# Refill loads of twice the size for experts two to seven of a soft MoE, with joined tiles

## The chip, the cores and the metric

The kernel runs on one core of a Trainium2 chip. The metric is the device time of one execution in microseconds (us). A core has five engines with one instruction queue each: TensorE (PE in the profile), VectorE (DVE), ScalarE (ACT), GpSimd (POOL) and SyncE (SP). SyncE computes nothing here: it issues every transfer of the kernel, in program order. The transfers themselves are carried by the core's 16 DMA engines.

## The reference

An attention with a sigmoid in place of the softmax feeds a soft mixture of experts. All data are float32.

```python
scores = q @ k.T / sqrt(64) - log(448)          # 8 batches, 12 heads, 448 tokens, 64 wide
x = (sigmoid(scores) @ v)                       # -> 3584 tokens x 768
logits = x @ phi                                # 768 -> 32 slots (8 experts x 4)
slot_input = softmax over tokens(logits).T @ x  # 32 x 768
for e in range(8):
    h = relu(slot_input[e] @ w1[e])             # 4 x 768 @ 768 x 1024
    slot_out[e] = h @ w2[e]                     # 4 x 1024 @ 1024 x 768
out = softmax over slots(logits) @ slot_out     # 3584 x 768
```

## The kernel before, in words

**Two parts.** For about 280 us TensorE computes the attention, batch after batch, and folds each finished batch of x into the slot inputs. Weights of the experts are loaded meanwhile, one or two units at a time. Then the experts run (`w1_part`, line 616; `w2_step`, line 730), and the output rows are made and stored (`out_half`, `out_rows`, `out_rows2`, lines 694 to 712).

**Units.** The weights come in 128 units of 128 partitions by 768 floats (3,072 bytes a partition): 64 of w1, eight per expert, and 64 of w2, two per call of `w2_step`. `units` (line 91) is the order in which they are loaded. The first 70 units, which hold all of w1 and six units of w2, are loaded during the attention. The other 58, all of w2, find no free room until w1 has been used: they are the refills, and they overwrite places that w1 (and the turned x, below) held.

**Places.** `slots` (line 98) lists the places in the order in which units take them, and later, in the same list, the order in which the output tiles take them. Before the change, a place `wa0` to `wa12` has four units. Besides there are `wpe` (four), `wpx` (two), `wpy` (four) and the tiles `wc` (two each).

**Refills.** `w1_part(e)` multiplies expert e by the two halves of its w1 (four units each). After each half it calls `load(4)` on the place that the half has just freed. The first refill goes into `wa0` in three pieces (lines 131 and 132), then come twelve loads of four units into `wa1` to `wa12`, one into `wpe`, all from the input `wq`, and one of two units into `wpx` from `wz`. A partition's line in `wq` is 12,288 bytes long. SyncE issues these loads, then the 23 stores of the output in program order.

**Who reads what.** Number the 32 calls of `w2_step` 0 to 31: 0 to 15 make the left half of the output's columns (pass 0), 16 to 31 the right half (pass 1). Step n reads two units. Steps 0 to 2 read the `wc` tiles. `wa0` holds the units of steps 3 and 4, `wa1` those of 5 and 6, and so on: `waN` those of 2N+3 and 2N+4, up to `wa12` with 27 and 28. `wpe` holds 29 and 30, `wpx` 31. Steps 20 to 27 are each followed by one `out_half` of the left half, which can run since `spread_sum` (line 721) has made pass 0's result ready after step 19. After step 31 the chain of line 718, `spread_sum` again, and the products of line 691 makes the other stores: two `out_rows`, five `out_rows2`, eight `out_half` of the right half.

**Turned x.** During the attention, the last 16 units' worth of the `wa` places hold not weights but the 32 by 32 transposed x (`yy`, line 165), and some columns for the slot softmax (`t1e`). Weights are loaded into them when the slot products (line 391) and line 418 have read them. `wpe` holds x and turned x of some batches (`xe`, `y0`, `y1`, line 171).

**Transfers in order.** A transfer waits at SyncE until its place is free. Each transfer raises one of eight semaphores in turn, so that the ninth transfer waits until the first has landed. This wait stands in the trace as SyncE at line 134 waiting for a DMA.

Of the kernel before, what the change touches and what calls it, by code (L numbers as in the profile page):

```python
# [9 lines left out]
F32 = mybir.dt.float32  # L10
# [7 lines left out]
DM, NSLOT, E, SPE, F = 768, 32, 8, 4, 1024  # L18
P = 128
# [10 lines left out]
UNIT = 768  # L30
N_A = 52
N_X = 16
N_1 = N_A - N_X + 2
N_C = 4
N_F = 70
# [22 lines left out]


@with_exitstack  # L60
def soft_moe_attention(ctx: ExitStack, tc: tile.TileContext, qk, v, vl, phi, w, wq, wz, cst, out):
    nc = tc.nc
    ctx.enter_context(tc.manual_schedule(engines=MANUAL))

# [2 lines left out]
    wpa = ctx.enter_context(tc.tile_pool(name="wpa", bufs=1))  # L67
# [23 lines left out]
    units = [(u1, u2)[m][n] for m, a, b in ORDER for n in range(a, b)]  # L91
    state = {"next": 0, "ring": 0, "used": 0, "room": 0, "wpb": None}
    utile, quads = {}, {}
    wpe, wpx, wpy = (wpa.tile([P, n * UNIT], F32, name=name) for name, n in (("wpe", 4), ("wpx", 2), ("wpy", 4)))

    wa_slots = [("wa", n, 0, 4) for n in range(N_A // 4)]
    n1 = (N_A - N_X) // 4
    slots = wa_slots[:n1] + [(wpy, 0, 0, 2)] + wa_slots[n1:] + [(wpe, 0, 0, 4), ("wc", 0, 0, 2), (wpx, 0, 0, 2)]
    slots += [("wc", n, 0, 2) for n in range(1, N_C)] + [(wpy, 0, 2, 4)]
    slots += wa_slots + [(wpe, 0, 0, 4), (wpx, 0, 0, 2), (wpy, 0, 0, 4)] + wa_slots  # L100

    def ring_tile(size=1):
        while state["used"] + size > state["room"]:
            pool, n, used, room = slots[state["ring"]]
            state.update(ring=state["ring"] + 1, used=used, room=room)
            if pool == "wa":
                pool = wpa.tile([P, 4 * UNIT], F32, name=f"wa{n}")
            elif pool == "wc":
                pool = state["wpb"].tile([P, 2 * UNIT], F32, name=f"wc{n}")
            state["tile"] = pool  # L110
        t = state["tile"][:, state["used"] * UNIT:(state["used"] + size) * UNIT]
        state["used"] += size
        return t

    def load(size):
        n = state["next"]
        if n >= len(units):
            return
        state["next"] = n + size
        if n < N_F:  # L120
            src, m = w[n // 2], n % 2 * UNIT
        elif n < len(units) - 2:
            src, m = wq[(n - N_F) // 4], 0
        else:
            src, m = wz[0], 0
        t = quads[(0, 0)] if n == N_F else ring_tile(size)
        if n < N_F and units[n][0] == "w1" and units[n][2] == 0 and units[n][1] < E - 1:
            quads[units[n][1:4:2]] = state["tile"]
        if n == N_F:
            state["ring"] += 1  # L130
            for a in range(0, 4 * UNIT, 4 * 256):
                nc.sync.dma_start(t[:, a:a + 4 * 256], src[:, a:a + 4 * 256])
        else:
            nc.sync.dma_start(t, src[:, m:m + size * UNIT])
        for k in range(size):
            utile[units[n + k]] = t[:, k * UNIT:(k + 1) * UNIT]
# [6 lines left out]
    def w1_mm(ph, e, kcs):  # L143
        for kc in kcs:
            for j in range(4):
                if e < E - 1:
                    wt = quads[(e, kc // TR)][:, (kc % TR * 4 + j) * 256:(kc % TR * 4 + j + 1) * 256]
                else:
                    wt = utile[("w1", e, j, kc // TR)][:, kc % TR * 256:(kc % TR + 1) * 256]
                nc.tensor.matmul(  # L150
                    ph[32 * j:32 * j + 32, 0:256], phi_sb[:, kc, :], wt,
                    start=(kc == 0), stop=(kc == NKC - 1))

    with ExitStack() as actx:
# [5 lines left out]
        def hold(kind, n=""):  # L160
            return ap.tile(kinds[kind], F32, name=f"{kind}{n}")

        wx = [wpa.tile([P, 4 * UNIT], F32, name=f"wa{(N_A - N_X) // 4 + n}") for n in range(N_X // 4)]
        ny = TR * NB2 * P
        yy = [w4[:, 0:ny].rearrange("p (k c f) -> p k c f", k=TR, c=NB2) for w4 in wx]
        t1e = [w4[:, ny:ny + NB2 * NSLOT + 1] for w4 in wx]
# [1 line left out]
        held = {k: hold(*k) for k in (("qk", 0), ("qk", 1), ("v", 0))}  # L168
        vlt = ap.tile([P, P], F32, name="vl")[:]
        held.update({k: hold(*k) for k in (("qk", 2), ("att", 0), ("att", 1), ("att", 2), ("v", 1))})  # L170
        yf = [wpe[:, 0:2 * UNIT], wpe[:, 2 * UNIT:4 * UNIT], wpy[:, 2 * UNIT:4 * UNIT]]
        xe = [y[:, 0:TR * S].rearrange("p (k s) -> p k s", k=TR) for y in yf]
        y0, y1, yn = (y.rearrange("p (k c f) -> p k c f", k=TR, c=NBK) for y in yf)
        xy = ap.tile([P, TR * NBK * P], F32, name="xy")
# [378 lines left out]
        for i in range(len(seq) + LAG):  # L553
            for f in early.get(i, ()):
                f()
            if i < len(seq):
                u = seq[i]
                score(u)
                if u[1] == NFK:
                    load_qk(u[0] + 3)  # L560
                elif u[0] % 2 == 1 and u[1] == NFK - 1:
                    load_qk(u[0] + 3)
                while state["next"] < min(N_1, (i + 1) * N_1 // W_STEPS):
                    load(1)
                if state["next"] < N_1 + N_X and (i > NX0 and i % 2 == 1 and state["next"] < N_1 + N_X // 2 or i > NX1):
                    load(1)
                if i == (B - 1) * per_b + LAG + LAST_S:
                    load(2)
                    load(2)
# [39 lines left out]
    def av_tile(name):  # L609
        turn[name] += 1  # L610
        return ps_av.tile([P, 512], F32, name=f"{name}{turn[name] % 2}")

    for _ in range(N_C + 2):
        load(2)

    def w1_part(e, ph=None):
        if ph is None:
            ph = av_tile("av0")
            w1_mm(ph, e, range(TR))
        if e < E - 1:  # L620
            load(4)
        if e == 0:
            finish(ps_t)
        w1_mm(ph, e, range(TR, NKC))
        load(min(4, len(units) - state["next"]))
        return ph

    def h_part(e, ph):
# [65 lines left out]
    def out_half(m, hf):  # L694
        ov = ring_tile().rearrange("p (j c) -> p j c", j=2)
        for j in range(2):
            out_tile(ov[:, j, :], m + j, hf, j)
        nc.sync.dma_start(
            out[m * ROWS:(m + 2) * ROWS, hf * HALF:(hf + 1) * HALF].rearrange("(j p) c -> p j c", p=P), ov)

    def out_rows(m):
        ov = ring_tile().rearrange("p (j c) -> p j c", j=2)
        for hf in range(2):
            out_tile(ov[:, hf, :], m, hf, hf)
        nc.sync.dma_start(out[m * ROWS:(m + 1) * ROWS, :].rearrange("p (j c) -> p j c", j=2), ov)
# [39 lines left out]
    for e in range(E):  # L745
        ph = w1_part(e, ph0 if e == 0 else None)
        if prev is not None:
            h_part(*prev)
        prev = (e, ph)
        combine_softmax(e)  # L750
# [67 lines left out]
```

## Time and profile before

| what | value |
|---|---|
| median of 3 runs | 370.95 us (370.52 to 371.78) |
| the profiled execution | 371.16 us |
| its span, first to last instruction | 369.4 us |
| TensorE busy in the span | 346.2 us (94%) |
| mean granted TensorE clock | 0.981 |
| HBM read, written | 83.59 MB, 11.01 MB |

The span is what the hardware profiler saw from the first to the last instruction of one execution. The profiled execution is 1.76 us longer than its span, and 0.21 us longer than the median. In the rows below, a time is counted from the start of the span. A line that begins with a start time is a merged piece of a timeline: start, duration, what it is, how many instructions, and in brackets what the engine was idle for just before. PE counts two records for one float32 matmul: one `w2_step` of four matmuls is `x8`.

### The profile page before, as it was taken

To read this page: it belongs to the slowest core of one execution; us is meant where nothing else is said; L and a number is where in the kernel's file an instruction comes from. 1 tells how busy PE (TensorE), PEld (TensorE's weight loads), DVE (VectorE), ACT (ScalarE), POOL (GpSimd) and SP (SyncE) were. 2 spreads that over 40 slices of the span, in tenths; PEclk is the share of its full clock that TensorE was granted. 3 is DMA by queue.
4 is the path that set the end of the run, shared out by engine and by line. 5 is a ranking of instruction groups with operands and counts; after the bars stand their busy time and mean duration, and the time that the engine had idled before them with its cause. 6 is when DMAs were issued, how large, how long until landed. Compare 5 with 4: busy or idle time off the path is not lost.

```text
span 369.4 us, 10332 instructions
## 1 busy us (share of the span) xinstructions
PE 346.2 (94%) x4315; PEld 172.0 (47%) x4315; DVE 241.2 (65%) x614; ACT 222.0 (60%) x305; POOL 8.2 (2%) x36
## 2 busy tenths in 40 slices
PE   9999999999999999999999999999999988996840
PEld 5566655644444355444444644464557643422520
DVE  0158829796894986769859695989746782141650
ACT  5777777577777765777777387747672114421540
POOL 1000000000000000000000000000102000100000
PEclk9999999999999999999999999999999999999895
DMA  7666566465677663766566388739689999999997
GB/s 230 222 217 209 182 221 217 141 216 172 211 227 219 201 199 98 227 212 197 190 215 230 92 293 262 238 110 373 231 285 369 428 421 422 424 422 405 395 409 282
DMA packets 34494, 95.27 MB, mean 258 GB/s; under 512 B 3600, under 2 KB 17296, under 8 KB 32784
## 3 DMA queue, kind: packets, MB, share of 16 engines
q1 hardware_dynamic: 34448, 94.62, 73.1%
q8 instruction: 34, 0.56, 0.6%
q14 instruction: 12, 0.10, 0.1%
HBM read 83.59 MB, written 11.01 MB: 256 GB/s over the span
## 4 chain that ended last, share of the span: by engine, by line
PE 78%; DMA 14%; DVE 3%; ACT 0%; issue 0%; DVEq 0%; ACTq 0%; SPq 0%
PE sc L234 34%; PE av L275 33%; DMA wpx<-in_wz_dram 8%; DMA wa<-in_wq_dram 6%; PE av L150 3%; PE sc L391 2%; PE sc L337 2%; DVE wa L692 2%; DMA qk<-in_qk_dram 1%; PE sc L319 1%; PE av L250 1%; PE pt L691 1%; PE av L391 0%; PE av L691 0%; PE av L723 0%
## 5 line engine op out<-in xcount | busy, mean ns | idle before, releaser
L242 ACT ACTIVATE att<-sc,sm 128x896 f32<-128x896 f32 x167 | 167.8, 1007 | 80.6 <-PE sc L234 77.3
L234 PE MATMUL sc<-qk 64*64 64x448 f32 x1336 | 180.0, 538 | 0.1
L275 PE MATMUL av<-att,v 64*64 64x448 f32 x1128 | 152.7, 537 | 0.0
L234 PEld LDWEIGHTS sc<-qk 64*64 64x64 f32 x1336 | 61.2, 133 | 71.0 <-issue 58.1
L275 PEld LDWEIGHTS av<-att,v 64*64 64x64 f32 x1128 | 54.5, 133 | 54.3 <-issue 52.6
L300 DVE STREAM_TRANSPOSE wa<-wpe 32x384 f32<-32x384 f32 (+5 forms) x144 | 58.0, 403 | 2.2
L300 DVE STREAM_TRANSPOSE wa<-xy 32x192 f32<-32x192 f32 (+3 forms) x96 | 33.1, 345 | 1.6
L282 DVE TENSOR_TENSOR wpe<-wpe,av 128x448 f32<-128x448 f32 x18 | 11.2, 621 | 31.3 <-PE av L275 20.1
L275 PE MATMUL av<-att,vl 64*64 64x448 f32 x188 | 26.4, 537 | 0.0
L300 DVE STREAM_TRANSPOSE wa<-wpx 32x288 f32<-32x288 f32 (+1 forms) x48 | 25.0, 520 | 0.8
L282 DVE TENSOR_TENSOR wpx<-wpx,av 128x448 f32<-128x448 f32 x15 | 9.3, 621 | 19.7 <-PE av L275 17.5
L150 PE MATMUL av<-wa,jt 128*32 128x256 f32 x312 | 17.2, 380 | 0.2
L692 ACT COPY wa<-av 128x384 f32<-128x384 f32 x24 | 10.9, 479 | 9.1 <-PE av L691 8.6
L692 DVE COPY wa<-pt 128x384 f32<-128x384 f32 x24 | 12.6, 555 | 5.5 <-PE pt L691 5.2
L282 DVE TENSOR_TENSOR xy<-xy,av 128x448 f32<-128x448 f32 x14 | 8.7, 622 | 8.2 <-ACT xy L278 4.1
L275 PEld LDWEIGHTS av<-att,vl 64*64 64x64 f32 x188 | 9.2, 133 | 9.2 <-issue 9.0
L150 PEld LDWEIGHTS av<-wa,jt 128*32 128x32 f32 x312 | 10.1, 110 | 6.7 <-issue 0.3
L691 PE MATMUL av<-lt,wc 128*128 128x384 f32 x28 | 12.5, 447 | 0.5 <-DVE lt L726 0.5
L691 PE MATMUL pt<-lt,wc 128*128 128x384 f32 x28 | 10.5, 377 | 1.1 <-DVE lt L726 1.1
L300 DVE STREAM_TRANSPOSE wpe<-xy 32x256 f32<-32x256 f32 (+3 forms) x32 | 11.0, 345 | 0.5
L633 ACT COPY t<-tmp 128x32 f32<-128x32 f32 x8 | 1.7, 217 | 15.7 <-DVE tmp L631 15.7
L740 PE MATMUL av<-wa,jt 128*32 128x384 f32 x104 | 10.2, 493 | 1.0 <-DMA wa<-in_wq_dram 1.0
(171 smaller groups left out, 262.8 us busy)
## 6 DMA issues: line engine op xcount, KB each, us to landing
qk<-in_qk_dram SPq DMA_DIRECT2D x47, 448.0 KB, 3.7
wa<-in_w_dram SPq DMA_DIRECT2D x52, 384.0 KB, 4.1
wa<-in_wq_dram SPq DMA_DIRECT2D x12, 1536.0 KB, 23.9
v<-in_v_dram SPq DMA_DIRECT2D x48, 192.0 KB, 2.6
out_dram<-wa SPq DMA_DIRECT2D x14, 384.0 KB, 7.0
out_dram<-wa SPq DMA_DIRECT2D x5, 768.0 KB, 6.3
wc<-in_w_dram SPq DMA_DIRECT2D x4, 768.0 KB, 6.3
vl<-in_vl_dram SPq DMA_DIRECT2D x24, 64.0 KB, 2.0
```

Of the source, the lines that this page charges most:

```text
L150: nc.tensor.matmul(ph[32 * j:32 * j + 32, 0:256], phi_sb[:, kc, :], wt, start=(kc == 0), stop=(kc == NKC - 1))
L234: nc.tensor.matmul(sc[h][64 * t:64 * t + 64, 0:S], qkts[pt][r, S + k0:S + k0 + 64], qkts[pt][r, 0:S], start=True, stop=True)
L242: nc.scalar.activation(att[:], tile2[:, :, 0:S], AF.Sigmoid, bias=nbias, scale=QSCALE)
L250: nc.tensor.matmul(o[k][r, 0:t.stop - t.start], w[:, r], att[:, h, t], start=start, stop=stop)
L275: nc.tensor.matmul(o[t][r, 0:S], w, att[row, h, :], start=start, stop=stop)
L282: nc.vector.tensor_tensor(out=x_of(p), in0=x_of(p), in1=av[0][:, 0:S], op=ALU.add)
L300: nc.vector.transpose(y[32 * g:32 * g + 32, k0:k0 + n, c0:c0 + m, BLK * a:BLK * a + BLK], src)
L337: nc.tensor.matmul(lg[32 * j:32 * j + 32, BLK * c0[j]:BLK * (c0[j] + n)], phi_sb[:, hp, :], blocks(x, j if x is xa else (j + 2) % 4, n), s ...
L391: nc.tensor.matmul(sls[t][32 * a:32 * a + 32, :], zt[:, c * BLK:(c + 1) * BLK], y_of(t, gi, c)[:, :, BLK * a:BLK * a + BLK], start=(c == 0 ...
L691: nc.tensor.matmul(pf[:, 0:HALF], ct_of(m, step), sts[hf], start=True, stop=True)
L692: (nc.scalar.copy, nc.vector.tensor_copy)[n % 2](ov, pf[:, 0:HALF])
L740: nc.tensor.matmul(po[32 * fl:32 * fl + 32, 0:HALF], h[:, k:k + NSLOT], ut, start=(n == 0), stop=(n == 2 * E - 1))
```

## The change

Experts 1 to 3 (the second to the fourth) get places of eight units (`wa2`, `wa3`, `wa4`) for both halves of their w1. Turned x gets two places of eight (`wa5`, `wa6`), whose halves take the part of the four tiles `wx`. `wpe` grows to eight units: its first half takes expert 4's first half of w1, its second half the x and turned x that `wpe` held, and later the last four units of expert 6. The refills into these six places are single loads of eight units from a new input `wo`, whose partition lines are 24,576 bytes long. The refill of `wa0` (three pieces) and of `wa1` (four units) stays, and so does the last one of two units. A refill of eight is issued when both halves that its place held have been multiplied. Bytes, order of the units and the arithmetic stay as they were: 13 loads of 12,288-byte lines beyond the pieces of `wa0` become one of these and six of 24,576-byte lines.

After the change `wa2` holds the units of steps 7 to 10, `wa3` of 11 to 14, `wa4` of 15 to 18, `wa5` of 19 to 22, `wa6` of 23 to 26, `wpe` of 27 to 30.

```diff
-    wpe, wpx, wpy = (wpa.tile([P, n * UNIT], F32, name=name) for name, n in (("wpe", 4), ("wpx", 2), ("wpy", 4)))
-
-    wa_slots = [("wa", n, 0, 4) for n in range(N_A // 4)]
-    n1 = (N_A - N_X) // 4
-    slots = wa_slots[:n1] + [(wpy, 0, 0, 2)] + wa_slots[n1:] + [(wpe, 0, 0, 4), ("wc", 0, 0, 2), (wpx, 0, 0, 2)]
+    wpe, wpx, wpy = (wpa.tile([P, n * UNIT], F32, name=name) for name, n in (("wpe", 8), ("wpx", 2), ("wpy", 4)))
+
+    first = [("wa", 0, 0, 4), ("wa", 1, 0, 4)] + [("wa", n, 0, 8) for n in range(2, 5)]
+    yslots = [("wa", n, 0, 8) for n in (5, 6)]
+    slots = first + [(wpe, 0, 0, 4), (wpy, 0, 0, 2)] + yslots + [(wpe, 0, 4, 8), ("wc", 0, 0, 2), (wpx, 0, 0, 2)]
     slots += [("wc", n, 0, 2) for n in range(1, N_C)] + [(wpy, 0, 2, 4)]
-    slots += wa_slots + [(wpe, 0, 0, 4), (wpx, 0, 0, 2), (wpy, 0, 0, 4)] + wa_slots
+    slots += first + yslots + [(wpe, 0, 0, 8), (wpx, 0, 0, 2), (wpy, 0, 0, 4)] + first
...
-                pool = wpa.tile([P, 4 * UNIT], F32, name=f"wa{n}")
+                pool = wpa.tile([P, room * UNIT], F32, name=f"wa{n}")
...
-            src, m = wq[(n - N_F) // 4], 0
+            src, m = (wq[(n - N_F) // 4] if size == 4 else wo[(n - N_F) // 8 - 1]), 0
...
-            quads[units[n][1:4:2]] = state["tile"]
+            k = state["used"] - size
+            quads[units[n][1:4:2]] = state["tile"][:, k * UNIT:(k + 4) * UNIT]
...
-        wx = [wpa.tile([P, 4 * UNIT], F32, name=f"wa{(N_A - N_X) // 4 + n}") for n in range(N_X // 4)]
+        w8 = [wpa.tile([P, 8 * UNIT], F32, name=f"wa{n}") for n in (5, 6)]
+        wx = [w[:, k * UNIT:(k + 4) * UNIT] for w in w8 for k in (0, 4)]
...
-        yf = [wpe[:, 0:2 * UNIT], wpe[:, 2 * UNIT:4 * UNIT], wpy[:, 2 * UNIT:4 * UNIT]]
+        yf = [wpe[:, 4 * UNIT:6 * UNIT], wpe[:, 6 * UNIT:8 * UNIT], wpy[:, 2 * UNIT:4 * UNIT]]
...
+    def refill(half):
+        size = {0: 4, 1: 4, 3: 8, 5: 8, 7: 8, 10: 8, 12: 8, 13: 8, 15: 2}.get(half)
+        if size:
+            load(size)
+
     def w1_part(e, ph=None):
...
-        if e < E - 1:
-            load(4)
+        refill(2 * e)
         if e == 0:
             finish(ps_t)
         w1_mm(ph, e, range(TR, NKC))
-        load(min(4, len(units) - state["next"]))
+        refill(2 * e + 1)
         return ph
...
-    wq = w[N_F // 2:-1].reshape(-1, 2, P, 2 * UNIT).transpose(0, 2, 1, 3).reshape(-1, P, 4 * UNIT)
+    wq, wo = (w[a:b].reshape(-1, n, P, 2 * UNIT).transpose(0, 2, 1, 3).reshape(-1, P, 2 * n * UNIT)
+              for a, b, n in ((N_F // 2, N_F // 2 + 4, 2), (N_F // 2 + 4, -1, 4)))
```

## Rows read from the trace of the kernel before

**Rows 1.** The span in 40 equal slices of 9.2 us: tenths of TensorE's busy time, tenths of the DMA engines' busy time, and what they moved in GB/s.

```profile
PE   9999999999999999999999999999999988996840
DMA  7666566465677663766566388739689999999997
GB/s 230 222 217 209 182 221 217 141 216 172 211 227 219 201 199 98 227 212 197 190 215 230 92 293 262 238 110 373 231 285 369 428 421 422 424 422 405 395 409 282
```

**Rows 2.** The chain of waits from 270 us to the end, in order of time: start, duration, what it was.

```profile
282.70 8.02 PE av L150 x144
290.72 0.02 issue
290.74 22.66 DMA wa<-in_wq_dram
...
313.46 27.73 DMA wpx<-in_wz_dram
341.19 0.04 issue
341.23 0.90 PE av L740 x8
```

**Rows 3.** TensorE's timeline in pass 1: steps 16 and 17 at 320.71, 18 and 19 at 322.02, the sum of pass 0 at 323.43, step 20 at 324.27, and so on to step 31 at 341.23.

```profile
318.60 1.50 PE L740 MATMUL av<-wa,jt 128*32 128x384 f32 x16
...
322.02 1.47 PE L740 MATMUL av<-wa,jt 128*32 128x384 f32 x16
323.43 0.91 PE L723 MATMUL av<-tmp,csb 128*128 128x384 f32 x2
324.27 0.85 PE L740 MATMUL av<-wa,hw 128*32 128x384 f32 x8
...
326.13 0.85 PE L740 MATMUL av<-wa,hw 128*32 128x384 f32 x8
...
328.79 0.85 PE L740 MATMUL av<-wa,jt 128*32 128x384 f32 x8
...
331.94 0.85 PE L740 MATMUL av<-wa,hw 128*32 128x384 f32 x8 [0.43 <-DMA wa<-in_wq_dram]
...
335.64 0.85 PE L740 MATMUL av<-wa,jt 128*32 128x384 f32 x8 [0.98 <-DMA wa<-in_wq_dram]
...
336.98 0.85 PE L740 MATMUL av<-wa,hw 128*32 128x384 f32 x8
339.34 0.85 PE L740 MATMUL av<-wpe,hw 128*32 128x384 f32 x8 [1.51 <-DMA wpe<-in_wq_dram]
340.01 0.83 PE L740 MATMUL av<-wpe,jt 128*32 128x384 f32 x8
```

**Rows 4.** SyncE's timeline, issues of refills and stores: start, duration, what it moves.

```profile
284.26 0.33 SPq L134 DMA_DIRECT2D wa<-in_wq_dram  x1
...
286.85 0.33 SPq L134 DMA_DIRECT2D wa<-in_wq_dram  x1
...
313.46 0.33 SPq L134 DMA_DIRECT2D wpx<-in_wz_dram  x1
326.87 5.66 SPq L698 DMA_DIRECT2D out_dram<-wpy  x4
...
341.26 0.47 SPq L698 DMA_DIRECT2D out_dram<-wa  x1
346.00 0.94 SPq L705 DMA_DIRECT2D out_dram<-wa  x2
```

**Rows 5.** The time from issue to landing of three transfers: the load issued at 284.26 (`wa1`), the one issued at 294.62 (`wa9`, steps 21 and 22), and the store issued at 341.26 (the last of the eight of the left half).

```profile
DMA to landing us min/median/max: 9.9/9.9/9.9
...
DMA to landing us min/median/max: 29.9/29.9/29.9
...
DMA to landing us min/median/max: 7.7/7.7/7.7
```

**Rows 6.** Stretches of the core from 344 to 350 us: the length, busy time and instructions of each engine, then TensorE's granted clock, the DMA engines' busy share, GB/s.

```profile
344.00:345.00 1.00, 0.11 (x1) 0.11 (x2) 0.80 (x2) 0.33 (x1) 0.00 (x0) 1.00 1.06 396
345.00:346.00 1.00, 1.00 (x4) 1.00 (x5) 0.58 (x2) 0.35 (x1) 0.00 (x0) 0.63 1.05 395
346.00:346.50 0.50, 0.50 (x3) 0.39 (x3) 0.50 (x1) 0.34 (x2) 0.00 (x0) 0.50 0.88 329
346.50:347.00 0.50, 0.50 (x3) 0.39 (x2) 0.42 (x2) 0.34 (x2) 0.00 (x0) 0.50 0.97 352
347.00:347.50 0.50, 0.50 (x3) 0.39 (x3) 0.42 (x2) 0.41 (x1) 0.00 (x0) 0.50 0.98 375
347.50:348.00 0.50, 0.50 (x4) 0.49 (x2) 0.42 (x2) 0.43 (x1) 0.00 (x0) 0.50 1.02 384
348.00:349.00 1.00, 1.00 (x5) 0.78 (x4) 0.92 (x2) 0.68 (x3) 0.00 (x0) 0.67 1.04 410
```

**Rows 7.** Line 418, the last reader of a group's turned x, and two issues of SyncE's timeline in the attention: the first load into a place of turned x of either pair.

```profile
L418 DVE SCALAR_TENSOR_TENSOR jt<-jt,wa,sc x2: 415/415/415, 207.2 to 243.7; 128x192 f32<-128x192 f32 x2
...
213.61 0.36 SPq L134 DMA_DIRECT2D wa<-in_w_dram  x1
...
246.25 0.86 SPq L134 DMA_DIRECT2D wa<-in_w_dram  x2
```

More of the change, by code (lines that the diff above doesn't have):

```diff
@@ L60, in soft_moe_attention @@
 @with_exitstack
-def soft_moe_attention(ctx: ExitStack, tc: tile.TileContext, qk, v, vl, phi, w, wq, wz, cst, out):
+def soft_moe_attention(ctx: ExitStack, tc: tile.TileContext, qk, v, vl, phi, w, wq, wo, wz, cst, out):
     nc = tc.nc
@@ L804 @@
     cst[:, 128:256] = ar[:, None] % NSLOT == ar[None, :] % NSLOT
-    host = {"qk": qk, "v": vv, "vl": vl, "phi": phi, "w": w, "wq": wq, "wz": wz, "cst": cst}
+    host = {"qk": qk, "v": vv, "vl": vl, "phi": phi, "w": w, "wq": wq, "wo": wo, "wz": wz, "cst": cst}
     nc = bacc.Bacc("TRN2", target_bir_lowering=False, num_devices=1, dynamic_dma_scratch_size=64)
```

## The prediction

> **What bounds the kernel now.** I read the slices first. TensorE is at 9 tenths up to about 277 us, while the DMA engines moved some 200 GB/s. From slice 31 on the DMA engines are at 9 tenths and above 390 GB/s to the last slice [rows 1]. So the attention is TensorE's and everything behind it belongs to the transfers. The chain of waits says the same: behind the w1 products come one refill and the last refill, whose landing at 313.46 + 27.73 = 341.19 releases step 31 [rows 2]. TensorE's timeline shows which step meets a landing: steps 25, 27, 29 and 31 begin when their load has landed, at 331.94, 335.64, 339.34 and 341.23; the others find their units there [rows 3]. The spacing is 3.70 us for a load of 1,536 KB, twice, and 341.19 - 339.30 = 1.89 us for the last one of 768 KB. The refills thus run back to back in the order of issue, and the stores stand behind them in the same order.
>
> The last look is at the hand-over to the stores. The eight stores of the left half are all issued by 341.26 [rows 4], and the last lands 7.7 us later, at 348.96 [rows 5]. The next store waits for the chain behind step 31 and leaves at 346.00 [rows 4]. In between the rate falls from 395 to 329 GB/s, then recovers by way of 352, 375 and 384 [rows 6]. So some of the 16 engines had finished their part of the eight stores and had nothing to do while others still worked on theirs. The loss is (66 + 43 + 20 + 11) x 0.5 / 395 = 0.18 us of all engines.
>
> **The attention: nothing.** The joined tiles could make a load wait for the reader of either half. For turned x that last reader is line 418, which begins at 207.2 and 243.7 and takes 0.42 us. The first loads into those places leave at 213.61 and 246.25 [rows 7], 6.0 and 2.1 us later, so the wider wait has been met. If that cover failed, SyncE's loads of q, k and v would queue behind it; that needs a slip over 2 us. Expert 4's half in the other end of `wpe` is only another address. I take 0; below nothing there is no reason for a gain, TensorE being busy.
>
> **Issue of the refills: nothing.** `wa2` waits for both halves of expert 1, so its load leaves when the load of `wa3` leaves now, at 286.85 [rows 4], and later ones fall 2.6 us apart or less. The engines have work from the loads before it until `wa1` lands at 284.26 + 9.9 = 294.2 [rows 4, 5]. So 7.3 us cover this wait. Each joined load then feeds the engines for 7.4 us, longer than the 2.6 us between issues. Fewer transfers also mean that SyncE issues its last refill well before the 313.46 of now; the first store leaves at 326.87 behind step 20's products in any case, so this gives nothing.
>
> **Longer lines: -0.48 us.** Going from 6,144 to 12,288 bytes a line takes 2 x 1.89 - 3.70 = 0.08 us off 1,536 KB. The trace has no line of 24,576 bytes. If the cost is one per line, the next doubling saves half as much, 0.04 us in each of the twelve old loads that are joined: 0.48 us. If it is one per transfer, six transfers fewer save 6 x 0.08 = 0.48 us too. Ends: 0 (the lines are cut again on their way) and 12 x 0.08 = 0.96 us (the saving repeats); a loss has no row that speaks for it, since twice the length was not slower. I take 0.48 and keep both ends. The steps see the part gathered so far: 0.32 us at `wa5`, 0.40 at `wa6`, 0.48 at `wpe` and `wpx`.
>
> The Trainium skill, in "DMA: Bandwidth & Descriptors", section "Anatomy of one DMA — SWDGE (gpsimd) path", gives each transfer a fixed 2.0 us beside its bytes, and by that alone six transfers fewer would be worth 12 us. The trace disagrees for transfers that queue: 3.70 us a load leaves 0.08 for anything fixed [rows 3], so the sum keeps 0.48.
>
> **Steps that now wait for two loads.** Step n starts when its whole joined load is there.
> - Steps 7 to 18: no wait. `wa4` (15 to 18) lands with the old `wa7`; two loads and 7.4 us before `wa9`, at 317.1, and step 15 runs at 318.60 + 0.67 = 319.3 [rows 3].
> - Step 19 ran at 322.02 + 0.67 = 322.69. `wa5` lands with the old `wa9`, at 294.62 + 29.9 = 324.5 [rows 5], less 0.32: 324.2. TensorE idles 1.5 us, and the sum of pass 0 and step 20 slip by as much, to about 325.8.
> - Steps 20 to 22 with their products take 1.33 us each (326.13 to 328.79 is two of them), so step 23 could run at about 330.3. It waits for `wa6`, the old `wa11`: 331.90 - 0.40 = 331.5. Steps 23 to 26 then end at 331.5 + 4 x 1.33 = 336.8.
> - Step 27 ran at 335.64 and now waits for `wpe`: 339.30 - 0.48 = 338.82. It carries the eighth `out_half`, so step 28 comes 1.34 later (335.64 to 336.98), and 29, 30 and 31 come 0.67 apart (339.34 to 340.01): 340.16, 340.83, 341.50, 342.17. Step 31 ran at 341.23. So the chain behind it slips by +0.94 us, and without the longer lines' gain by 1.42: steps 27 and 28 stand behind the last but one landing instead of ahead of it.
>
> The slipped stores of steps 20 to 27 cost nothing: they stand behind the refills in any case. The eighth needs step 27's products, ready some 2 us after 338.8; it leaves now at 341.26.
>
> **What reaches the end: +0.4 us.** The engines get to the end of the eight stores 0.48 us earlier, and the next store leaves 0.94 later, at 346.94: 1.42 us of wider gap. I take them to run dry evenly over the 2.9 us or so between 346.0 and 348.96 [rows 5, 6]. Then a gap of length t costs t x t / 5.8 of all engines; today's 0.18 us is t = 1.0. With t = 2.4 it is 1.0 us, 0.8 more. Minus 0.48 saved: +0.3 to +0.4, and I take +0.4 since the last engine, not the mean one, sets the end. Bounds: 0 - 0.48 where the late engines set the end alone, and 0.94 where the whole slip passes.
>
> Sum: 371.16 + 0.4 = 371.56 for the profiled execution; that one is 0.21 us over the median, so 371.35 beside 370.95, say 371.4.
>
> **The rivals.** A difference under 0.3% (1.1 us) can't be told from none in a measurement of this kernel.
> - *The clock falls in the new gap (slower).* From 336.8 to 338.8 TensorE now idles 2.0 us, against 1.51 before step 29 today [rows 3]. The granted clock is 1.00 up to 345, 0.63 in 345 to 346, 0.50 in 346 to 348, and 0.67 in the next us [rows 6]. So it falls to the lower of its two levels (1.2 instead of 2.4 GHz) about 345.3, behind a us in which TensorE was busy 0.11 us, and stays there for some 3.4 us. A fall during steps 27 to 31 would put about 1.7 us of their work at half speed: +1.7 on the chain. Then all engines run dry and the end moves by about 0.94 + 1.7 - 0.5 = 2.1: 373.0. For it: steps 27 to 31 are now in one piece right behind the longest gap. Against: gaps of 0.98 and 1.51 close together did not do it today. It decides once the gap before step 27 brings on the lower clock ahead of step 31.
> - *The whole slip passes, without any gain from the lines.* 1.42 us at the end: 372.4. For it: the first store behind the gap is one all others follow. Against: 329 of 395 GB/s flowed on in today's gap [rows 6].
> - *The slip is hidden.* If the engine that is last at 348.96 sets the end, it never runs dry (346.94 lies well before it), and the gain of the lines is left: -0.48, 370.5. Against: the last engine at 349 needn't be the last at 368.
> - *Each transfer has a price of its own that the queue doesn't hide (faster).* Six fewer then bring `wpe` forward by six prices. For over 0.3% the price has to pass 0.25 us a transfer (1.5 us earlier, so that the slip goes too and 1.1 us is left at the end: 369.8). Against: the spacing of 3.70 and 1.89 us leaves at most 0.08 [rows 2, 3]. By the fixed 2.0 us of the Trainium skill's section named above the time would be some 12 us less, about 359.
> - *The change doesn't do what it says:* lines cut again. The chain slips 1.42, the gap costs 0.8 and saves nothing: 371.8. This lies inside the forecast's own range.
>
> **How the numbers follow.** Forecast with its bounds (370.9 to 372.0): 0.50. Clock: 0.18. Whole slip: 0.15. Hidden slip: 0.12. A price of each transfer: 0.05. Slower by over 0.3% (above 372.06): the clock, most of the whole slip and the forecast's edge, 0.34. Faster (below 369.84): that price and a sliver of the hidden slip, 0.06. Within: 0.60. The range reaches from under the hidden slip to the clock's case, 370.3 to 373.0.
>
> **What would show it.** In the changed profile TensorE should wait for a DMA before steps 19, 23 and 27 alone, about 1.5, 1.2 and 2.0 us, and step 31 should run without a wait, about 342.2. Joined loads should be 7.36 us apart. The first `out_rows` store should leave about 346.9, and the dip behind 346 should be deeper and longer, near 1 us of all engines. The prediction is wrong if the attention ends later than 281, if joined loads land further apart than 7.4, if the clock falls before step 31, or if the dip grows and the end doesn't move.

## The result, and the profile after

The changed kernel is slower: 373.53 us (median of 7 runs, 372.07 to 374.73) beside 371.13 us for the kernel before, measured with it (370.41 to 372.23). The ratio is 1.0058, with a 95% interval of 1.0042 to 1.0074. The forecast was 371.4 us and no difference. The time lies outside the range and close to the rival called slower, which stood at 373.0.

The execution that was profiled is the shortest of the seven: 372.07 us, a span of 370.3. It must not be taken for the median. It shows the transfers and the waits as the change makes them, but not, as the experiments will show, what most executions pay. In the changed kernel line 691 has become 697, 740 is 746, the copies behind 691 are at 698, and the loads are issued at 135. In the kernels of the experiments the same lines can stand a few lines lower (746 is 750 in split_last, for instance).

TensorE's timeline of the changed kernel, from step 18 on (steps 18 and 19 at 324.06, step 23 at 331.76, 27 at 339.08, 28 and 29 at 340.41, 31 at 342.37), beside [rows 3]:

```profile
324.06 1.47 PE L746 MATMUL av<-wa,jt 128*32 128x384 f32 x16
...
331.76 0.85 PE L746 MATMUL av<-wa,jt 128*32 128x384 f32 x8 [0.88 <-DMA wa<-in_wo_dram]
...
335.75 0.85 PE L746 MATMUL av<-wa,jt 128*32 128x384 f32 x8
336.53 0.44 PE L697 MATMUL av<-lt,wc 128*128 128x384 f32 x1
336.81 0.34 PE L697 MATMUL pt<-lt,wc 128*128 128x384 f32 x1
339.08 0.85 PE L746 MATMUL av<-wpe,jt 128*32 128x384 f32 x8 [1.94 <-DMA wpe<-in_wo_dram]
...
340.41 1.50 PE L746 MATMUL av<-wpe,hw 128*32 128x384 f32 x16
341.73 0.83 PE L746 MATMUL av<-wpe,jt 128*32 128x384 f32 x8
342.37 0.83 PE L746 MATMUL av<-wpx,jt 128*32 128x384 f32 x8
```

The joined loads land 339.08 - 331.76 = 7.32 us apart, against 2 x 3.70 in [rows 3]: 0.08 us less for each. `wpe` is there at 339.04, 0.26 us earlier than in [rows 2, 3]. Step 27 now stands behind that landing. Step 31 no longer waits for its own load, but runs at 342.37 in place of 341.23: the slip is 1.14 us, 0.94 having been forecast. The first `out_rows` store leaves at 347.11, 1.11 us later than before (forecast 346.9).

The chain of waits confirms which transfer that is. It is no longer the last refill [rows 2] but the joined one before it, issued at 300.31 and landing 38.73 us later:

```profile
283.14 17.15 PE av L151 x312
300.29 0.02 issue
300.31 38.73 DMA wpe<-in_wo_dram
339.04 0.04 issue
339.08 0.85 PE av L746 x8
```

The hand-over to the stores, in the columns of [rows 6]:

```profile
346.00:346.50 0.50, 0.49 (x3) 0.49 (x4) 0.01 (x1) 0.00 (x0) 0.00 (x0) 1.00 0.86 323
346.50:347.00 0.50, 0.50 (x4) 0.34 (x2) 0.50 (x2) 0.34 (x1) 0.00 (x0) 1.00 0.74 266
347.00:347.50 0.50, 0.46 (x3) 0.30 (x2) 0.50 (x3) 0.50 (x2) 0.00 (x0) 1.00 0.53 200
347.50:348.00 0.50, 0.50 (x4) 0.32 (x3) 0.50 (x3) 0.34 (x2) 0.00 (x0) 1.00 0.51 194
```

Against 395 GB/s these four stretches lose (72 + 129 + 195 + 201) x 0.5 / 395 = 0.76 us of all DMA engines, where it was 0.18. So far the mechanism is the one forecast: 0.58 us more of empty engines, about 0.26 us of earlier landings, and 372.07 against 371.16 in the two profiled executions. These 0.91 us are more than the 0.32 that the two terms leave, and under the 0.94 of the whole slip. Executions of one kernel differ by more than that (370.41 to 372.23 before), so this pair doesn't tell which of the two it is.

What does not fit is the rest: six of seven executions took 373.48 us or more, 1.4 to 2.7 above the profiled one. Three theories were put to the test. Theory A: in most executions the clock falls in the gap ahead of step 27, as the rival said. Theory B: the slip passes whole to the end, with a fall of the clock only behind step 31. Theory C: joined loads are slower in other executions.

### The profile page after: what moved, and what is told of

Its sections match the earlier page's. It is cut to its first block, busy times and chain, and to the rows that moved or that the text cites. A ratio compares the mean times of both kernels' runs of the same rounds, so it can differ in the third digit from the quotient of the medians.

```text
span 370.3 us, 10314 instructions
## 1 busy us (share of the span) xinstructions
PE 347.2 (94%) x4315; PEld 173.8 (47%) x4315; DVE 240.9 (65%) x614; ACT 221.8 (60%) x305; POOL 8.2 (2%) x36
## 4 chain that ended last, share of the span: by engine, by line
PE 81%; DMA 12%; DVE 2%; ACT 0%; issue 0%; ACTq 0%; DVEq 0%
PE sc L236 34%; PE av L277 33%; DMA wpe<-in_wo_dram 10%; PE av L151 5%; PE sc L393 2%; PE sc L339 2%; DVE wa L698 1%; DMA out_dram<-wa 1%; PE av L746 1%; DMA qk<-in_qk_dram 1%; PE sc L321 1%; PE av L252 1%; PE av L393 0%; PE av L697 0%; PE pt L697 0%; PE av L729 0%
## 5 line engine op out<-in xcount | busy, mean ns | idle before, releaser
L236 PEld LDWEIGHTS sc<-qk 64*64 64x64 f32 x1336 | 62.7, 133 | 74.5 <-issue 61.6
L277 PEld LDWEIGHTS av<-att,v 64*64 64x64 f32 x1128 | 53.6, 133 | 55.4 <-issue 53.4
L151 PE MATMUL av<-wa,jt 128*32 128x256 f32 x288 | 16.3, 380 | 0.2
L151 PEld LDWEIGHTS av<-wa,jt 128*32 128x32 f32 x288 | 13.9, 110 | 1.7 <-issue 0.3
L697 PE MATMUL pt<-lt,wc 128*128 128x384 f32 x28 | 9.5, 341 | 1.1 <-DVE lt L732 1.1
```

The costliest lines, as they stand in the source:

```text
L151: nc.tensor.matmul(ph[32 * j:32 * j + 32, 0:256], phi_sb[:, kc, :], wt, start=(kc == 0), stop=(kc == NKC - 1))
L236: nc.tensor.matmul(sc[h][64 * t:64 * t + 64, 0:S], qkts[pt][r, S + k0:S + k0 + 64], qkts[pt][r, 0:S], start=True, stop=True)
L277: nc.tensor.matmul(o[t][r, 0:S], w, att[row, h, :], start=start, stop=stop)
L697: nc.tensor.matmul(pf[:, 0:HALF], ct_of(m, step), sts[hf], start=True, stop=True)
```

## The experiments

All times are medians. Each is given with its ratio to the kernel before, measured with it on the same chip, and the 95% interval of the ratio.

**again: the changed kernel once more,** with no edit, for a profile of another execution.

> The changed kernel once more, nothing left out. Theory A (the clock falls in TensorE's gap before step 27 in most executions, though not in the profiled one of 372.07 us): the median is about 373.5 again, executions differ by 1 to 2.5 us, the longer ones have the lower mean clock, and a profile of an execution above 373 shows the lower clock inside 339 to 344 us with steps 27 to 31 at up to double length. Theory B (the slip of the chain behind step 31 passes whole to the end, the clock falls only behind step 31 and slows the products of the stores): the low stretch begins at 345 or later and steps 27 to 31 keep 0.67 us. Theory C (joined loads are slower in other executions): they land further apart than the 7.31 us of the profile.

The median is 373.86 us, a ratio of 1.0057 (1.0040 to 1.0075). The profiled execution took 373.49 this time. Its timeline and its stretches (in the columns of [rows 6]) from the gap on:

```profile
338.91 0.85 PE L746 MATMUL av<-wpe,jt 128*32 128x384 f32 x8 [1.94 <-DMA wpe<-in_wo_dram]
...
340.39 2.79 PE L746 MATMUL av<-wpe,hw 128*32 128x384 f32 x16
342.96 1.05 PE L746 MATMUL av<-wpe,jt 128*32 128x384 f32 x8
343.83 0.82 PE L746 MATMUL av<-wpx,jt 128*32 128x384 f32 x8
```

```profile
338.00:340.00 2.00, 1.09 (x10) 0.46 (x10) 0.00 (x0) 0.00 (x0) 0.07 (x1) 1.00 0.98 392
340.00:342.00 2.00, 2.00 (x14) 0.60 (x16) 0.56 (x1) 0.48 (x1) 0.14 (x1) 0.50 1.03 385
342.00:344.00 2.00, 2.00 (x20) 0.64 (x16) 0.00 (x0) 0.00 (x0) 0.00 (x0) 0.65 1.07 401
344.00:346.00 2.00, 1.34 (x12) 0.49 (x3) 0.00 (x0) 0.48 (x1) 0.00 (x0) 1.00 1.06 397
```

The gap is the same 1.94 us and step 27 starts 0.17 us earlier than in the first profile. Then the granted clock is 0.50 from 340 on, the lower of the two levels (1.2 GHz), and back at the higher one before 344. Steps 28 and 29 take 2.79 us in place of 1.50. From the start of step 27 to that of step 31 it is 343.83 - 338.91 = 4.92 us instead of 342.37 - 339.08 = 3.29, so 1.63 us more. Step 31 is 1.46 us later than in the first profile, and that goes through to the end: 373.49 against 372.07 is 1.42. The joined loads land 7.32 us apart again (338.91 - 331.59, the starts of steps 27 and 23). That is Theory A; B had the fall at 345 or later, C the landings. One part of A's expectation is wrong: the mean clock of an execution says little (0.980 here too), since a fall elsewhere, hidden, counts the same. The first profile had one at 307.8 (its clock is 0.72 from 306 to 312), under steps of pass 0 that found their loads long landed.

**warm_gap: the gap filled.**

```diff
     for n in range(2 * E):
+        if n == 11:
+            pd = ps_t.tile([P, 512], F32, name="pt")
+            for _ in range(7):
+                nc.tensor.matmul(pd[:, 0:P], ident, ident, start=True, stop=True)
         w2_step(po, 1, n)
```

Here `n == 11` is step 27, since `n` counts the steps of pass 1 from 16.

> The changed kernel with seven more 128-column products into an unread tile ahead of step 27, so that TensorE works through most of the 1.94 us gap; nothing is left out. Theory A: the lower clock no longer comes ahead of step 31, and the median falls to that of the execution without it, 372.0 (-1.5 from the changed kernel). Theories B and C: no change, 373.5.

The median is 371.88 us, a ratio of 1.0007 (0.9995 to 1.0020), and no execution is above 372.66. Work that nobody reads takes 2 us off. In its timeline the seven products (x14) leave 0.37 us of the gap, and steps 28 and 29 keep 1.50:

```profile
336.83 1.72 PE L773 MATMUL pt<-csb 128*128 128x128 f32 x14
338.93 0.85 PE L746 MATMUL av<-wpe,jt 128*32 128x384 f32 x8 [0.37 <-DMA wpe<-in_wo_dram]
...
340.25 1.50 PE L746 MATMUL av<-wpe,hw 128*32 128x384 f32 x16
341.57 0.83 PE L746 MATMUL av<-wpe,jt 128*32 128x384 f32 x8
342.21 0.83 PE L746 MATMUL av<-wpx,jt 128*32 128x384 f32 x8
```

Step 31 still runs at 342.21, 0.98 us later than before. So the slip is there without the loss, against Theory B, and so are the joined loads, against Theory C.

**warm_early and warm_23: the same elsewhere.** The diff is that of warm_gap, with seven products at `n == 0` (step 16), and with three at `n == 7` (step 23).

> The control for warm_gap: the changed kernel with the same seven products, but ahead of step 16, some 15 us before the gap; nothing is left out. They shift steps 16 to 22 by 1.5 us into the wait before step 23, and leave the gap before step 27 at about 1.9 us. Theory A (the lower clock during steps 27 to 31, brought on by that gap): 373.5 as in the changed kernel. If the products help for another reason than filling this gap (a tile's rotation, any more work on TensorE): 372 as in warm_gap.

> A control that leaves the gap before step 27 as it is: the changed kernel with three products ahead of step 23 alone, inside its wait of 0.9 us; nothing is left out. Theory A (the gap of 1.94 us before step 27 brings on the lower clock in most executions): 373.5, single executions from 372 to 374.7. If any added product helps: 372.

warm_early failed as a control. It took 372.55 us, a ratio of 1.0034 (1.0018 to 1.0050), with executions from 371.77 to 374.76. In its profile pass 0 was late by a fall at 308, as in the first profile. Step 23 did not wait there, so the whole shift reached the gap and left 0.89 us of it:

```profile
338.81 0.85 PE L746 MATMUL av<-wpe,jt 128*32 128x384 f32 x8 [0.89 <-DMA wpe<-in_wo_dram]
```

It is a half dose rather than a control. warm_23 is the control that held. It took 373.93 us, a ratio of 1.0061 (1.0043 to 1.0079), with three added products but the gap untouched, and steps 28 and 29 slow again:

```profile
339.24 0.85 PE L746 MATMUL av<-wpe,jt 128*32 128x384 f32 x8 [1.94 <-DMA wpe<-in_wo_dram]
...
340.77 2.79 PE L746 MATMUL av<-wpe,hw 128*32 128x384 f32 x16
343.33 1.00 PE L746 MATMUL av<-wpe,jt 128*32 128x384 f32 x8
```

**warm_half: part of the gap.** The diff is that of warm_gap with three products in place of seven.

> The changed kernel with three products ahead of step 27, so that about 1.2 us of its gap stay; nothing is left out. Theory A: fewer executions fall to the lower clock than of the changed kernel, the median lies between 371.9 (warm_gap) and 373.5, and single executions still reach 373.5. A step at a length of the gap would show as all or nothing.

It took 372.52 us, a ratio of 1.0022 (1.0012 to 1.0031), with 1.28 us of the gap left in its profile. The same three products ahead of step 23 gave 373.93 (warm_23), so it matters where they stand and not that they are there. No execution was above 372.94, where up to 373.5 was expected. The profiled one keeps the clock up to step 31 and loses it at 347.05. So whether the fall ahead of step 31 still happens in part of these executions isn't shown; the median lies between, as expected.

**split_last, join_last, split_all: which of the joined loads.** The refills named issue two loads of four units from the same lines of the new input, back to back:

```diff
-        if size:
+        if size == 8 and half in (13,):
+            load(4)
+            load(4)
+        elif size:
             load(size)
```

This is split_last; join_last has `(3, 5, 7, 10, 12)` in place of `(13,)`, split_all all six. A second edit, left out here, gives each load of four units its columns in `wo`.

> The changed kernel with the last joined load (wpe, steps 27 to 30) issued as two of four units; the other five stay joined. Steps 27 and 28 then stand ahead of the last but one landing again. Theories A and B: the slip of 1.14 us on step 31 goes and the earlier landings of about 0.25 us stay: 370.9, a little under the kernel before (371.1). Theory C: the five joined loads still cost, so about 373.

> The changed kernel with the first five joined loads issued as two of four units each, and only wpe joined. Step 26 then ends near 334.7 and step 27 waits until 339.2, a gap of 4.5 us in place of 1.94. Theory A: the clock falls in nearly every execution, 373.8 or more, and the profile shows it. Theory B: slip alone, 372.4. Theory C: one joined load in place of six, about 371.6.

> The changed kernel's tiles and its new input, but all six joined loads issued as two of four units: lines of 12,288 bytes, places and moments of issue as changed. If the tiles or the new input cost anything it shows here: above 371.8 (the kernel before in the runs so far). If not: 371.8, and then split_last's 371.4 is what ten longer lines' loads gain, 0.3 to 0.4 us.

| kernel | joined | median, us | ratio (95%) |
|---|---|---|---|
| split_all | none | 371.75 | 1.0000 (0.9990 to 1.0011) |
| split_last | all but `wpe` | 371.38 | 0.9990 (0.9979 to 1.0001) |
| join_last | `wpe` alone | 373.86 | 1.0054 (1.0030 to 1.0078) |

So the joined tiles, the new input and the later issue cost nothing that can be measured, nor do five joined loads, and one of the six, the last, brings the whole loss. In split_last TensorE runs steps 27 to 30 with no wait for a DMA, and step 31 again waits 0.44 us for its own load, as in [rows 3]:

```profile
337.40 0.85 PE L750 MATMUL av<-wpe,jt 128*32 128x384 f32 x8
...
338.72 1.62 PE L750 MATMUL av<-wpe,hw 128*32 128x384 f32 x16
340.16 0.83 PE L750 MATMUL av<-wpe,jt 128*32 128x384 f32 x8
341.43 0.85 PE L750 MATMUL av<-wpx,jt 128*32 128x384 f32 x8 [0.44 <-DMA wpx<-in_wz_dram]
```

join_last's median is as expected. Its profiled execution, 371.76 us, is not: the gap is 2.70 us in place of 4.5, since pass 0 was late by a hidden fall there too (its clock is 0.72 from 306 to 312), and no fall follows the gap:

```profile
339.02 0.85 PE L750 MATMUL av<-wpe,jt 128*32 128x384 f32 x8 [2.70 <-DMA wpe<-in_wo_dram]
...
340.35 1.50 PE L750 MATMUL av<-wpe,hw 128*32 128x384 f32 x16
```

Its other seven executions took 372.33 to 375.12. No profile shows whether the clock fell in them.

**join_warm: join_last with its gap filled.** Ten products at `n == 11`, as in warm_gap.

> join_last (wpe alone joined; 373.86) with ten products ahead of step 27 in its gap of 2.7 us; nothing is left out. Theory A: the clock stays up and the median falls to the price of the slip alone, 372.0 to 372.3 (0.2 to 0.4 over warm_gap, since five loads keep the shorter lines). If the gap's clock isn't it: 373.9.

This was a miss: 373.22 us, a ratio of 1.0040 (1.0027 to 1.0053). The direction is right, the size is not. In the profiled execution the last refills landed late, and 1.46 us of the gap stayed open behind the products:

```profile
336.56 2.39 PE L777 MATMUL pt<-csb 128*128 128x128 f32 x20
340.42 0.85 PE L750 MATMUL av<-wpe,jt 128*32 128x384 f32 x8 [1.46 <-DMA wpe<-in_wo_dram]
```

The clock held there, and the time was 373.13 all the same, 1.4 us over join_last's profiled execution. Step 27 was late by the same 1.4 us (340.42 against 339.02). The products didn't do that: the load of `wpe` already left 1.28 us later (307.10 against 305.82), long before the first of them at 336.56. So landings moved by over a us between these two executions, and a fixed number of products is a weak cover. How much of join_warm's rest is clock and how much landing stays open, and with it what the clock costs join_last.

**warm_before, best and best_again.** warm_before is the kernel before with three products ahead of step 27 and five ahead of step 29. best is split_last with such products in three other gaps; `fill(k)`, whose definition is left out here, issues k of them into an unread tile:

```diff
+        fill({7: 3}.get(n, 0))
         w2_step(po, 1, n)
...
-    spread_sum(gather(po))
+    so = gather(po)
+    fill(2)
+    spread_sum(so)
+    fill(4)
```

> The kernel before with three such products ahead of step 27 and five ahead of step 29, its two longest gaps (0.98 and 1.51 us); nothing is left out. If the clock falls there too in some executions: the median falls by 0.2 to 0.5 us from 371.8 and the upper end of the executions (372.8) comes down. If gaps of this length do nothing: 371.8.

> split_last with three products ahead of step 23 (a gap of 1.1 us), two behind step 31 and four ahead of the last products, so that TensorE's clock does not fall before the stores of the second half; nothing is left out. Theory A: the products behind step 31 keep 0.18 us each in place of 0.32, the second and third store behind the gap leave up to 1 us earlier, and as the DMA engines are short of work then, the end gains 0.2 to 0.5 us: about 371.0, under both kernels. If the transfers alone set the end: 371.4.

> The kernel of the run best once more, nothing left out, to see whether five joined loads with no gap ahead of step 27 are a gain that can be told from none. If they are: a ratio of 0.999 again, 0.3 to 0.5 us under the kernel before, with an interval that with the first one's leaves 1.000 out. If the first reading was chance: 1.000.

warm_before took 371.69 us, a ratio of 1.0004 (0.9992 to 1.0015). The gaps of 0.98 and 1.51 us of the kernel before cost it nothing that can be measured. best took 371.31 us, 0.9990 (0.9978 to 1.0002), and best_again 371.25 us, 0.9991 (0.9975 to 1.0007). The products behind step 31 kept the clock at 1.00 from 344 to 352 in best's profile, where split_last's fell to 0.50 at 345.5, and added nothing to split_last's ratio. So a fall behind step 31 shows no price here. Three readings of 0.999, of two kernels, speak for 0.3 to 0.4 us gained by five longer loads, about what the shorter landings are worth, but each interval by itself holds 1.000. A gain is likely but not shown.

## Why the prediction was wrong

- **The attention and the issue: right.** split_all, with the joined tiles, is at 1.0000.
- **Longer lines, -0.48 us at `wpe`: right in the spacing, not seen at the landing.** 7.32 us a joined load gives 6 x 0.08 = 0.48. The 7.36 named under what would show it did not follow from that sum; 7.32 does. `wpe` itself was there 0.26 and 0.43 us earlier in the two profiles of the changed kernel (339.04 and 338.87 for 339.30), and since landings move more than that between executions, the lines' part in it can't be told. Nothing came of the rival of a price of each transfer, which needed 1.5 us or more there. The section of the Trainium skill that the prediction sets beside it is headed for the gpsimd path, and SyncE issues all of these transfers.
- **Which steps wait: right in place.** In the first profile 0.88 and 1.94 us ahead of steps 23 and 27 (forecast 1.2 and 2.0). Step 19 did not wait there, since the hidden fall at 307.8 had made pass 0 late. In the run again steps 19 and 23 waited 0.63 and 1.11 us (forecast 1.5 and 1.2).
- **The slip, +0.94 us: 1.14 measured** in the first profile, because `wpe` was there at 339.04 and not at 338.82.
- **What reaches the end, +0.4 us: not contradicted without the clock.** warm_gap, which has slip and lines but not the fall, is at 1.0007, or 0.3 us, with an interval from -0.2 to 0.7. The dip was 0.76 us of all engines, forecast near 1.
- **The step that failed is the chance of the rival "The clock falls in the new gap".** Its place and its price were right: +1.7 us forecast on the chain, 1.63 measured; and 2.1 us at the end, where 2.40 and 2.09 were measured over the kernel before. But the sum took the clock at nothing, and the rival was given 0.18, on the argument that "gaps of 0.98 and 1.51 close together did not do it today". That was one execution's answer, at a shorter gap, taken as if it settled what a gap of 2.0 us does in all of them. Nor is the new gap the longest: the same trace has one of 2.47 us ahead of 306.10, with no fall behind it, and in the first profile after the change one of 2.40 at the same place did bring a fall (see the end). So one profile gives no odds. The runs put in its place that a gap of 1.94 us ahead of step 27 brings the lower clock in most executions. Two profiles show the fall itself (again and warm_23); for the others only the time speaks: only one of the thirteen of the changed kernel stayed under 373 us. With the gap filled all twelve did, and with the gap left and products elsewhere none of six.
- **The range** ended at 373.0, the rival's own middle. It left nothing for the spread of executions within that case, nor for that of the kernel before, whose median was 370.95 in three executions and 371.77 in twenty-five others.

## What to carry to other kernels

Joining two loads delays the user of the first half until the second has landed; where loads run back to back, that is free as long as the user comes later than that, and the last join before a chain is where it wasn't. Here five early joins cost nothing and gained about 0.1% if anything, while the last cost 0.5%. So look at the last join first, and leave that load small where its user waits for it. A gap that a join opens in TensorE's work can be priced twice: by its own length, and by the half-speed stretch that may follow it; if the work behind it is on the path, look at several executions, since one profile may show either case.

## What the runs showed that was not expected

The same gap of 1.94 us brought the lower clock in one profile and not in the other, and a gap of 2.70 us passed without it. A longer gap stands in every profile here: 2.4 to 2.5 us ahead of the first products of line 668 (674 after the change), behind steps 0 and 1. The first two lines are of the kernel before, the gap and the stretch with it (in the columns of [rows 6]); the last is the same stretch in the first profile after the change:

```profile
306.10 0.65 PE L668 MATMUL pt<-csb,tmp 128*128 128x128 f32 x4 [2.47 <-ACT tmp L660]
306.00:312.00 6.00, 5.90 (x59) 2.40 (x59) 1.54 (x6) 2.86 (x8) 0.42 (x2) 1.00 1.02 427
...
306.00:312.00 6.00, 5.45 (x39) 1.94 (x39) 1.03 (x4) 2.29 (x6) 0.21 (x1) 0.72 0.99 426
```

Of the fourteen profiles eight have a clock of 0.72 in this stretch and six 1.00, and the changed kernel itself has one of each (0.72 in the first, 1.00 in again). So the length of a gap alone doesn't decide. Four profiles have 1.94 us or more open ahead of step 27. In two of them the clock fell at about 307 and not at 340 (the first one and join_last), in the other two at 340 and not at 307 (again and warm_23). Four are too few to tell whether the one keeps off the other.

Where the clock fell ahead of step 31, the way from step 27 to step 31 took 4.92 us in both profiles that show it (again and warm_23), in place of 3.29. Seven unread products of 128 columns, 1.72 us of TensorE's time, were worth 373.86 - 371.88 = 2.0 us.
